# Layer 1's second set: second products by seven of eight instead of all eight

## The chip, the cores and the metric

The kernel runs on one core of a Trainium2 chip. The metric is the time of one execution on the device in microseconds (us); of several runs the median counts. The core's engines are TensorE (PE in the profile: matmuls; PEld: its weight loads), VectorE (DVE), ScalarE (ACT), GpSimd (POOL) and SyncE (SP), which here only issues transfers. Each engine works through its own queue in order and waits at an instruction whose operands are not there.

## The reference

A random-feature attention is followed by two gated layers:

```python
q_p, k_p = phi(q * scale), phi(k * scale)         # phi: exp(x @ omega.T - |x|^2/2 - max) / sqrt(m)
num = q_p @ (k_p.T @ v);  den = q_p @ k_p.sum(seq) + 1e-6
x = (num / den)                                   # 4 batches x 576 rows = 2304 rows, 8 heads x 64 = 512 columns
x = (silu(x @ w_gate) * (x @ w_val)) @ w_out      # layer 1: 512 -> 1536 -> 512
x = (sigmoid(x @ w_gate2) * (x @ w_val2)) @ w_out2  # layer 2, the same sizes
```

The weights come as float64 and are converted to float32 on the chip.

## The kernel before, in words

**Sets and stages.** Of the 2304 rows, 4 x 512 are handled as two *sets* of two batches each; the 4 x 64 rows left over ("R", 256 columns) go along with one set of each layer. Layers are numbered 0 and 1 in the code, so (0,0), (0,1), (1,0), (1,1) are (layer, set), in the order of the program (`LARGE`); (0,0) and (1,1) carry the leftover rows. In this text layer 1 of the title is layer 0 of the code. `big(l, n, ...)` does one set: six *blocks* p of 256 columns of d_ff, each of seven *slots* k (the first products, gate and value together), then the second products with w_out, then, for (0,0) and (1,1), twelve short slots of leftover rows.

**Seven of eight.** A product of 2 x 2 blocks needs eight block products; with sums of blocks formed beforehand on both sides (Strassen's scheme in Winograd's form) seven suffice. The first products of all four sets are done so: slots k0 to k6 accumulate in PSUM banks X, Z, X, Y, X, Z, X. For the second products there are two functions: `eight()`, twelve slots of 24 matmuls, and `seven()`, 21 slots; the tuple `SEVEN = (1, 0), (1, 1)` says which sets use `seven()`. There the left sums s1 to s4 of the hidden values are formed by `form_s1` to `form_s4` during the blocks before, and the right sums of w_out come from DRAM.

**Every product is three.** A float32 operand is split into a high part (ACT: `vh`, `xhi`, `hh`) and the rest (DVE: `vl`, `xlo`, `hl`), and `three` (L420 to L424) issues high x high, low x high, high x low.

**Weights.** Class `Weight` loads a 128 x 1024 piece of float64 words (`raw64`, by POOL's queue once attention is over) and turns it into float32: `magnitude` (L186, ACT), `bits` (L194), `power` (L201), `term` (L207) and `total` (L215, sometimes a POOL transfer instead), all DVE. A pair of pieces then gives block sums in `sums` (L273: four DVE operations 256 wide), and pieces and sums are stored to DRAM (`w_first`, `w_out`, `w_diff`) by SP. `make()` is this work as a generator. Later each slot fetches its 256 KB from there (`fetch`, SP, tile `wp`), three to five slots ahead, and splits it three slots ahead: `prepare_hi` (L407, ACT) and `prepare_lo` (L411, DVE).

**The order.** The program is written in the order in which each engine shall work. After the matmuls of each slot `step()` (L972) advances a clock, runs what `after(n, ...)` had put off, prepares the slot three ahead, and then takes conversions from `make()` according to a credit (`SHARES`, `room`, `needs`). At k4 and k5 `total` (L1021) adds PSUM sums on DVE, one slot later `gate` (L991) has ACT take the activation and DVE multiply. In the first block after a set whose second products go by `seven()`, the operand sums of x that are needed in slots 3 and later (`x_jobs`, `X_LATE`) are formed within that block; otherwise all of them are formed beforehand. Attention's order is a table of names, `START`.

Of the kernel before, what the change touches and what calls it, by code (L numbers as in the profile page):

```python
# [28 lines left out]
ld.0 mk.0 mq.0 nk.0 tK.0 tQ.0 hQ.0 hK.0 mr.0 ld.1 sr.0 load0.0 lv.0 tR.0 sk.0 hR.0 pK.0 pQ.0 mk.1  # L29
nq.0 lR.0 xK0.0 pR.0 mr.1 ld.2 gK0.0 bK0.0 xK1.0 gK1.0 bK1.0 mq.1 eK0.0 tK.1 sq.0 hK.1 load0.1 eK1.0  # L30
xQ0.0 nk.1 sk.1 gQ0.0 bQ0.0 xQ1.0 gQ1.0 tR.1 hR.1 bQ1.0 magnitude0.0 lv.1 sr.1 eQ0.0 load1.0 eQ1.0
pK.1 lR.1 magnitude1.0 kv.0 xK0.1 q0.0 bits0.0 tQ.1 q2.0 bits1.0 gK0.1 nq.1 bK0.1 ke.0 c0.0 pR.1
load1.1 c2.0 q1.0 mk.2 nA.0 hQ.1 xK1.1 tK.2 gK1.1 dA.0 load0.2 sq.1 lv.2 eK0.1 bK1.1 c1.0 hK.2 pQ.1
iA.0 power0.0 yA.0 power1.0 eK1.1 magnitude0.1 mr.2 mq.2 magnitude1.1 nB.0 xQ0.1 gQ0.1 nk.2 term1.0
bQ0.1 tR.2 sk.2 hR.2 sr.2 dB.0 ld.3 xQ1.1
# [20 lines left out]
LEAD = 3  # L56
EARLY_UNITS = 12
FULL = (4, 5, 6, None)
SPENT = 0.6
# [4 lines left out]
SEVEN = (1, 0), (1, 1)  # L64
X_LATE = 3
LEAD7 = 3

SHARES = ((1, 1, 1, 1), (1, 1, 1, 1), 0.2, 7)
# [8 lines left out]
def tile_performer_attention__then__two_glu_layers(  # L77
# [25 lines left out]
    nc = tc.nc  # L103
    P = 128
# [48 lines left out]
    class Weight:  # L153
# [36 lines left out]
        def bits(self):  # L190
            if self.cast:
                self.place()
                r = self.res.bitcast(U32)
                nc.vector.tensor_scalar(  # L194
                    r, self.mag.bitcast(U32), 3, None, ALU.logical_shift_left
                )

        def power(self):

            if self.cast:  # L200
                nc.vector.tensor_scalar(  # L201
# [9 lines left out]
        def total(self, dma=False):  # L211
            if self.cast and dma:
                nc.gpsimd.dma_start(out=self.res, in_=self.mag, accum_op=ALU.add)
            elif self.cast:
                nc.vector.tensor_tensor(self.res, self.res, self.mag, ALU.add)  # L215

    loader = [nc.sync]
    units = []
    for l in range(2):
        units += [Weight(l, c + i, n) for c in range(0, FC, 2) for n in range(2) for i in range(2)]  # L220
        units += [Weight(l, c, 2) for c in range(FC)]

# [5 lines left out]
    w_diff = dram.tile([P, 4, FC // 2, H2], F32, name="wd")  # L228
# [5 lines left out]
    def put(u, v=None, t=None):  # L234
# [12 lines left out]
        for at, src in (  # L247
# [5 lines left out]
            store(dst[:, at], src)  # L253

    def sums(u, v, t):
# [16 lines left out]
        for dst, l, r, op in right if u.key[2] == 2 else left:  # L272
            nc.vector.tensor_tensor(dst, l, r, op)  # L273
# [24 lines left out]
    for l, n, small in LARGE:  # L298
        for p in range(FC // 2):
            for slot, product, r in slots(l, n, small, p):  # L300
# [3 lines left out]
                vector.append(9 if full else 0.6 + {4: 1.8, 5: 1.8, 6: 0.6, None: 0.6}.get(product, 0))  # L304
# [25 lines left out]
    def x_sum(s, name, later):  # L330
# [8 lines left out]
        elif s == 1 and xt["late"]:  # L339
# [5 lines left out]
        for kk in range(2):  # L345
            nc.vector.tensor_tensor(t[kk], l[kk], r[kk], ALU.subtract)
# [1070 lines left out]
```

## Time and profile before

| | us |
|---|---|
| three runs | 983.75, 986.4, 989.13 (median 986.4) |
| the profiled execution: its time | 983.23 |
| its span (first to last instruction) | 981.3 |
| PE busy | 970.5 (99%) |
| DVE busy | 771.1 (79%) |
| ACT busy | 609.4 (62%) |
| POOL busy | 87.4 (9%) |

TensorE's granted clock is 1.000 over the whole span. The time of an execution is its span and some 2 us around it. A busy row says how long instructions of a group lasted, which is longer than the distance from one to the next where they follow each other closely, since an instruction's end overlaps the start of the next; the timeline with its start times tells the distance.

The stages by the trace's matmuls, in us from the span's start: attention to 163.6; (0,0) first products to 312.5, second products to 378.0, leftover rows to 395.3; (0,1) first products to 509.6, second products to 574.9; (1,0) first products to 689.1, second products to 750.75; (1,1) to the end.

### The profile page before, as it was taken

Reading aid. Unit: us, or ns where it says so; the run is one execution under the profiler, and the core shown is the slowest. Engines: PE = TensorE matmul, PEld = TensorE weight load, DVE = VectorE, ACT = ScalarE, POOL = GpSimd, SP = SyncE. Lnnn points to the kernel's source line nnn. Section 1 sums busy time; section 2 is a strip of 40 time slices with the busy share of each in tenths; the row PEclk is TensorE's granted clock in tenths of the full one; section 3 lists DMA queues with packets and bytes.
Section 4 is the critical chain, followed back from the end, with each engine's and each line's share of the span. In section 5 each row is a group of like instructions: output and inputs, shape, how many; then the busy total and the mean of one; then the engine's idle time right before and its main releaser. Section 6 shows DMA issues by size and latency. Waiting matters only on the chain.

```text
span 981.3 us, 16934 instructions
## 1 busy us (share of the span) xinstructions
PE 970.5 (99%) x5929; PEld 854.6 (87%) x5929; DVE 771.1 (79%) x1584; ACT 609.4 (62%) x1295; POOL 87.4 (9%) x130
## 2 busy tenths in 40 slices
PE   8999999999999999999999999999999999999998
PEld 7999998888888889888888888888999888889996
DVE  6898999888887899778888878856986655557674
ACT  7999998655554456555555465554775544445763
POOL 2222112011010100001000000000100000000200
PEclk9999999999999999999999999999999999999999
DMA  7657766577786666777765566543464322223754
GB/s 221 169 139 190 213 190 190 163 235 251 251 277 195 184 205 207 246 226 229 229 198 151 177 203 220 155 126 97 107 169 142 109 86 86 85 84 91 161 151 129
DMA packets 129913, 170.23 MB, mean 173 GB/s; under 512 B 32420, under 2 KB 83108, under 8 KB 129828
## 3 DMA queue, kind: packets, MB, share of 16 engines
q1 hardware_dynamic: 117392, 131.43, 44.3%
q0 software_dynamic: 11952, 37.49, 13.8%
q8 instruction: 46, 0.75, 0.3%
q14 instruction: 39, 0.32, 0.1%
q10 hardware_dynamic: 484, 0.23, 0.1%
HBM read 123.76 MB, written 39.32 MB: 166 GB/s over the span
## 4 chain that ended last, share of the span: by engine, by line
PE 92%; DVE 3%; ACT 2%; DMA 1%; issue 0%; ACTq 0%; SPq 0%; DVEq 0%
PE X L422 12%; PE X L424 12%; PE X L423 12%; PE Z L424 6%; PE Z L422 6%; PE Z L423 6%; PE Y L424 4%; PE Y L422 4%; PE Y L423 4%; PE p L644 3%; PE o L698 2%; PE R L424 2%; PE R L423 2%; PE R L422 2%; PE acc L422 2%; PE acc L423 2%
## 5 line engine op out<-in xcount | busy, mean ns | idle before, releaser
L411 DVE TENSOR_TENSOR vl<-wp,vh 128x512 fp32r<-128x512 f32 x274 | 188.2, 689 | 144.3 <-ACT vh L407 142.2
L407 ACT ACTIVATE vh<-wp 128x512 fp32r<-128x512 f32 x274 | 169.9, 623 | 7.8 <-PE X L424 3.1
L422 PE MATMUL X<-xhi,vh 128*128 128x512 f32 x372 | 145.2, 390 | 0.1
L423 PE MATMUL X<-xlo,vh 128*128 128x512 f32 x372 | 145.0, 390 | 0.0
L424 PE MATMUL X<-xhi,vl 128*128 128x512 f32 x372 | 144.7, 389 | 0.0
L424 PEld LDWEIGHTS X<-xhi,vl 128*128 128x128 f32 x372 | 69.8, 188 | 14.7
L422 PEld LDWEIGHTS X<-xhi,vh 128*128 128x128 f32 x372 | 69.9, 188 | 14.2 <-DVE o L1196 0.3
L423 PEld LDWEIGHTS X<-xlo,vh 128*128 128x128 f32 x372 | 69.9, 188 | 13.7
L422 PE MATMUL Z<-xhi,vh 128*128 128x512 f32 x184 | 71.6, 389 | 0.0
L423 PE MATMUL Z<-xlo,vh 128*128 128x512 f32 x184 | 71.6, 389 | 0.0
L424 PE MATMUL Z<-xhi,vl 128*128 128x512 f32 x184 | 71.6, 389 | 0.0
L994 ACT ACTIVATE g<-h 128x512 f32<-128x512 f32 x28 | 17.7, 632 | 64.5 <-DVE h L1024 64.5
L1019 ACT ACTIVATE Y<-X 128x512 f32<-128x512 f32 x52 | 30.2, 584 | 40.4 <-PE X L424 40.0
L424 PE MATMUL X<-vh,hl 128*128 128x256 f32 x192 | 54.4, 284 | 0.0
L424 PE MATMUL R<-xr,vl 128*128 128x256 f32 x192 | 54.3, 283 | 0.0
L423 PE MATMUL X<-vl,hh 128*128 128x256 f32 x192 | 54.3, 283 | 0.0
L422 PE MATMUL X<-vh,hh 128*128 128x256 f32 x192 | 54.3, 283 | 0.0
L423 PE MATMUL R<-xr,vh 128*128 128x256 f32 x192 | 54.3, 283 | 0.0
L422 PE MATMUL R<-xr,vh 128*128 128x256 f32 x192 | 54.2, 282 | 0.0
L207 DVE SCALAR_TENSOR_TENSOR mag<-raw,mag 128x512 f32<-128x512 uint32 x72 | 49.5, 688 | 1.2
L186 ACT ACTIVATE mag<-raw 128x512 f32<-128x512 f32 x72 | 48.6, 676 | 1.4 <-DMA raw<-in_moe_w_val_dram 1.1
L215 DVE TENSOR_TENSOR res<-res,mag 128x512 f32<-128x512 f32 x61 | 42.0, 688 | 1.0
(244 smaller groups left out, 2621.5 us busy)
## 6 DMA issues: line engine op xcount, KB each, us to landing
wp<-wf SPq DMA_DIRECT2D x184, 256.0 KB, 3.0
wp<-ws SPq DMA_DIRECT2D x66, 256.0 KB, 2.9
wf<-res SPq DMA_DIRECT2D x48, 256.0 KB, 3.7
wf<-wsums SPq DMA_DIRECT2D x48, 256.0 KB, 4.0
raw<-in_moe_w_out_dram POOLq DMA_DIRECT2D x24, 512.0 KB, 4.2
raw<-in_moe_w_gate_dram POOLq DMA_DIRECT2D x18, 512.0 KB, 5.1
raw<-in_moe_w_val_dram POOLq DMA_DIRECT2D x18, 512.0 KB, 4.4
ws<-res SPq DMA_DIRECT2D x24, 256.0 KB, 3.8
```

Of the source, the lines that this page charges most:

```text
L186: nc.scalar.activation(self.mag, self.hi.bitcast(F32), AF.Prelu, scale=REBIAS, alpha=NEGATIVE)
L207: nc.vector.scalar_tensor_tensor(self.mag, self.lo, 2.0**-52, self.mag, ALU.mult, ALU.mult)
L215: nc.vector.tensor_tensor(self.res, self.res, self.mag, ALU.add)
L407: nc.scalar.activation(hi, fetched[o], AF.Copy)
L411: nc.vector.tensor_tensor(lo, fetched.pop(o), hi.bitcast(F32), ALU.subtract)
L422: nc.tensor.matmul(o, lhsT=l[0], rhs=r[0], start=start, stop=False, **kw)
L423: nc.tensor.matmul(o, lhsT=l[0], rhs=r[1], start=False, stop=False, **kw)
L424: nc.tensor.matmul(o, lhsT=l[1], rhs=r[0], start=False, stop=stop, **kw)
L644: nc.tensor.matmul(pj[a][:, i, :], lhsT=x[hs, i, :], rhs=wdf[hs, a, :], start=True, stop=True)
L698: nc.tensor.matmul(self.kv[:, h], lhsT=lhsT, rhs=rhs, start=n == 0, stop=n == 2 * NB)
L994: nc.scalar.activation(g, src[0], AF.Sigmoid if l else AF.Silu)
L1019: nc.scalar.activation(d, s, AF.Copy)
```

## The change

`SEVEN` gets (0, 1), so layer 1's second set uses `seven()`: 21 slots of 12 matmuls 512 wide in place of 12 slots of 24. What this needs elsewhere:

- the right sums of layer 1's w_out: a class `Again` loads its twelve pieces (256 KB each) from DRAM once more by SP, two at a time, and makes four sums of each pair on DVE and stores them (24 operations, 12 stores); in program order this stands in slots s1 to s8 of (0,0)'s second products. `w_diff` exists once per layer;
- the left sums: `form_s1` becomes an ACT copy and an accumulating POOL transfer except in (1,1); `form_s2` and `form_s3` stay on DVE, `form_s4` a POOL transfer; results go into `xx`, the input of layer 2;
- conversions pause from block 4, slot 4 of (0,1) to the end of its second products (`PAUSE`), since `seven()` uses their tiles. What is due for layer 2 is done earlier or later;
- the x sums for slots 3 and later of (1,0) move into that set's first block;
- each DVE instruction is counted into an estimate of what VectorE still has to do (`Counted`, `ahead`); `step` takes conversions only where it is under `BACKLOG` = 7.0, and under `TIGHT` = 0.3 ahead of slot k4;
- `split` is divided: its DVE half comes after `step`; `total` for k4 and k5 stays ahead of it (`TOTAL_FIRST`);
- `START` is written anew, and the leftover rows of attention's first pair of heads (`kqrem`) are loaded by SP behind `qraw`, not by ACT's queue.

```diff
-SEVEN = (1, 0), (1, 1)
+SEVEN = (0, 1), (1, 0), (1, 1)
+TIGHT = {4: 0.3}
+S1_DMA = True
+PAUSE = 4, 4
+BACKLOG = 7.0
+TOTAL_FIRST = (4,5)
-SHARES = ((1, 1, 1, 1), (1, 1, 1, 1), 0.2, 7)
+SHARES = ((1,0.8,1,1),(1,1,1,1),0.2,7)
...
+            def call(out, *args, **kw):
...
+                quick = name in ("tensor_scalar", "tensor_copy")
+                ahead[0] += n / (1920.0 if quick else 960.0) + 0.07
+                return f(out, *args, **kw)
...
+        def load(self):
+            self.pair = []
+            for i in range(2):
+                u = Weight(0, self.c + i, 2)
+                u.place()
+                nc.sync.dma_start(out=u.res, in_=w_out[0][:, self.c + i])
+                self.pair.append(u)
...
-                    if self.n == 0 and n == 0:
+                    if self.n == 0 and n == 1:
                         for i, rest in enumerate((k, q)):
-                            nc.scalar.dma_start(out=self.r[:, i, :], in_=rest[0, :2, MAIN:, :])
+                            nc.sync.dma_start(out=self.r[:, i, :], in_=rest[0, :2, MAIN:, :])
...
+            while pausing and u not in begun_units:
+                yield "clean"
...
-        room.append(share * max(2.74 * x - SPENT * y, 0.1))
+        room.append((kind != "t" or l) and share * max(2.74 * x - SPENT * y, 0.1))
...
-        while credit >= 1:
+        ahead[0] = max(0.0, ahead[0] - 2.72 * weight[o - 1])
+        limit = BACKLOG
+        if o < len(sequence) and sequence[o][0] == "f" and sequence[o][3] in TIGHT:
+            limit = TIGHT[sequence[o][3]]
+        while credit >= 1 and ahead[0] < limit:
...
+            if S1_DMA and not (l and n):
+                nc.scalar.activation(s1[p], a21, AF.Copy)
+                nc.gpsimd.dma_start(out=s1[p], in_=a22, accum_op=ALU.add)
+                return
...
-                        for m in range(4):
+                        for i in range(2 - 2 * l):
+                            three(
+                                dst[i],
+                                [u[:, p % 2 * H2 + i * P:p % 2 * H2 + (i + 1) * P] for u in w],
+                                now,
...
+                        for m in range(4 * l):
...
+                    if k in (4, 5):
+                        t = hold[k - 3][i]
+                        vec.tensor_tensor(t if k == 4 and i else to, dst[i], t, ALU.add)
```

How the change moves instructions, at three places. In the changed kernel all operations of VectorE go through one wrapper and so have its line, L124.

SP's queue at the program's start (`kraw`, `qraw`: keys and queries of a pair of heads; `kqrem`: their leftover rows). Before:

```order
L540 DMA kraw_171<-in_k_dram 128x2x256
L540 DMA qraw_175<-in_q_dram 128x2x256
L540 DMA kraw_199<-in_k_dram 128x2x256
L540 DMA qraw_201<-in_q_dram 128x2x256
L549 DMA kqrem_170<-in_k_dram 64x3x64 x2
```

and now:

```order
L586 DMA kraw_172<-in_k_dram 128x2x256
L586 DMA qraw_174<-in_q_dram 128x2x256
L590 DMA kqrem_171<-in_k_dram 128x1x64
L590 DMA kqrem_171<-in_q_dram 128x1x64
L586 DMA kraw_187<-in_k_dram 128x2x256
L586 DMA qraw_189<-in_q_dram 128x2x256
```

The first pair's `kqrem` stands between the first and the second pair's large loads; before, it stood on ACT's queue, behind `omega`.

VectorE in (0,1), block 2, from behind the `vl` made in slot k4 to the one made in slot k5 (`res`, `mag`: conversion; `wsums`: block sums; `hs`: a left sum; `h`: hidden values). Before:

```order
L273 TENSOR_TENSOR wsums_6105<-res_5891,res_6021 128x256
L273 TENSOR_TENSOR wsums_6105<-res_5891,wsums_6104 128x256
L1024 TENSOR_TENSOR h_6068<-Z_5997,h_6068 128x512
L1024 TENSOR_TENSOR h_5879<-Z_5998,h_5879 128x512
L999 TENSOR_TENSOR h_5999<-g_6123,h_5999 128x512
L411 TENSOR_TENSOR vl_6151<-wp_6075,vh_6150 128x512
```

and now:

```order
L124 TENSOR_SCALAR mag_6152<-res_6154 128x512
L124 SCALAR_TENSOR_TENSOR mag_6152<-raw64_6088,mag_6152 128x512
L124 TENSOR_TENSOR res_6154<-res_6154,mag_6152 128x512
L124 TENSOR_TENSOR wsums_6209<-res_6120 128x256
L124 TENSOR_TENSOR wsums_6209<-wsums_6209,res_6057 128x256
L124 TENSOR_TENSOR hs_6001<-h_5728,h_5859 128x512
L124 TENSOR_TENSOR h_6134<-Z_6064,h_6134 128x512
L124 TENSOR_TENSOR h_5929<-Z_6065,h_5929 128x512
L124 TENSOR_TENSOR h_6066<-g_6194,h_6066 128x512
L124 TENSOR_TENSOR vl_6232<-wp_6145,vh_6231 128x512
```

Three conversion steps and a left sum have come in ahead of the totals from Z.

VectorE in (1,0), block 0, slots k2 and k3 (`xt`: operand sums of x, `xlo`: their low parts). Before:

```order
L201 TENSOR_SCALAR mag_7374<-res_7376 128x512
L207 SCALAR_TENSOR_TENSOR mag_7374<-raw64_7243,mag_7374 128x512
L411 TENSOR_TENSOR vl_7418<-wp_7324,vh_7417 128x512
L215 TENSOR_TENSOR res_7376<-res_7376,mag_7374 128x512
L273 TENSOR_TENSOR wsums_7426<-res_7240 128x256
L273 TENSOR_TENSOR wsums_7426<-wsums_7426,res_7327 128x256
L411 TENSOR_TENSOR vl_7445<-wp_7368,vh_7444 128x512
```

and now:

```order
L124 TENSOR_SCALAR mag_7494<-res_7496 128x512
L124 SCALAR_TENSOR_TENSOR mag_7494<-raw64_6560,mag_7494 128x512
L124 TENSOR_TENSOR xlo_7551<-xx_80,xhi_7549 128x512
L124 TENSOR_TENSOR xlo_7555<-xx_80,xhi_7553 128x512
L124 TENSOR_TENSOR vl_7558<-wp_7453,vh_7557 128x512
L124 TENSOR_TENSOR res_7496<-res_7496,mag_7494 128x512
L124 TENSOR_SCALAR res_7566<-mag_7564 128x512
L124 TENSOR_TENSOR xt_7580<-xx_80,xt_7161 128x512
L124 TENSOR_TENSOR xt_7580<-xx_80,xt_7162 128x512
L124 TENSOR_TENSOR xlo_7585<-xt_7580,xhi_7583 128x512
L124 TENSOR_TENSOR xlo_7589<-xt_7580,xhi_7587 128x512
L124 TENSOR_TENSOR vl_7594<-wp_7492,vh_7593 128x512
```

The sums of x and their splitting now stand in this block, and conversion runs beside them.

Counted over a whole block from the two listings, VectorE has these instructions (wide: 512, other than TENSOR_SCALAR; narrow: 256 wide, or a TENSOR_SCALAR 512 wide):

| block | before: wide + narrow | now: wide + narrow |
|---|---|---|
| (0,0) block 1 | 26 + 17 | 26 + 19 |
| (0,1) block 1 | 19 + 10 | 23 + 14 |
| (0,1) block 2 | 19 + 10 | 24 + 14 |
| (0,1) block 3 | 20 + 9 | 24 + 12 |
| (0,1) block 4 | 20 + 10 | 23 + 14 |
| (0,1) block 5 | 19 + 7, and 2 of 1024 | 20 + 4 |
| (1,0) block 0 | 18 + 11 | 32 + 6 |
| (1,0) block 1 | 24 + 9 | 23 + 14 |
| (1,0) block 2 | 22 + 9 | 24 + 13 |
| (1,0) block 3 | 18 + 2 | 24 + 13 |
| (1,0) block 4 | 18 + 0 | 20 + 10 |
| (0,0) second products | 52 + 27, and 11 of 1024 | 41 + 32, and 11 of 1024 |
| (0,1) second products | 49 + 28, and 10 of 1024 | 78 + 0 |

Two TENSOR_SCALARs stand for one conversion: before, (0,0)'s second products hold 18 of them and (0,1)'s first products 27; now 6 and 33.

## Rows read from the trace of the kernel before

**Rows 1.** The page: span, busy time of the engines, the chain by engine.

```profile
span 981.3 us, 16934 instructions
PE 970.5 (99%) x5929; PEld 854.6 (87%) x5929; DVE 771.1 (79%) x1584; ACT 609.4 (62%) x1295; POOL 87.4 (9%) x130
PE 92%; DVE 3%; ACT 2%; DMA 1%; issue 0%; ACTq 0%; SPq 0%; DVEq 0%
```

**Rows 2.** Windows by stage: length, busy us by engine, clock, DMA share, GB/s.

```profile
163.60:312.50 148.90, 148.27 (x789) 128.18 (x789) 130.47 (x245) 82.79 (x154) 14.61 (x22) 1.00 0.73 232
...
378.00:395.30 17.30, 17.30 (x146) 17.26 (x144) 15.85 (x29) 11.24 (x20) 1.50 (x2) 1.00 0.84 263
395.30:509.50 114.20, 114.20 (x506) 94.60 (x505) 93.49 (x172) 67.20 (x121) 10.53 (x14) 1.00 0.73 230
...
574.90:689.00 114.10, 114.10 (x505) 94.53 (x504) 85.30 (x149) 63.62 (x115) 2.33 (x4) 1.00 0.52 161
689.00:750.75 61.75, 61.62 (x506) 60.68 (x505) 51.52 (x84) 42.53 (x77) 5.21 (x6) 1.00 0.56 146
```

**Rows 3.** Windows: (0,1) block 2.

```profile
433.40:452.40 19.00, 19.00 (x85) 15.76 (x84) 15.85 (x31) 10.91 (x21) 1.57 (x2) 1.00 0.72 228
```

**Rows 4.** Timeline of PE: each stage's first matmul; at 602.50 (1,0) block 1, k3.

```profile
509.57 0.39 PE L422 MATMUL X<-hh,vh 128*128 128x512 f32 x1
...
574.85 0.39 PE L422 MATMUL X<-xhi,vh 128*128 128x512 f32 x1
...
602.50 0.39 PE L424 MATMUL Y<-xhi,vl 128*128 128x512 f32 x1
...
689.09 0.28 PE L422 MATMUL X<-vh,hh 128*128 128x256 f32 x1
...
750.75 0.50 PE L422 MATMUL X<-xhi,vh 128*128 128x512 f32 x1
```

**Rows 5.** Timeline of DVE in (1,0): start, duration; in brackets idle before and its end.

```profile
595.62 0.69 DVE L215 TENSOR_TENSOR res<-res,mag 128x512 f32<-128x512 f32 x1
596.23 0.42 DVE L194 TENSOR_SCALAR res<-mag 128x512 uint32<-128x512 uint32 x1
596.56 0.68 DVE L999 TENSOR_TENSOR h<-g,X 128x512 f32<-128x512 f32 x1
597.95 0.69 DVE L411 TENSOR_TENSOR vl<-wp,vh 128x512 fp32r<-128x512 f32 x1 [0.71 <-ACT vh L407]
598.56 0.42 DVE L201 TENSOR_SCALAR mag<-res 128x512 uint32<-128x512 uint32 x1
599.02 0.69 DVE L207 SCALAR_TENSOR_TENSOR mag<-raw,mag 128x512 f32<-128x512 uint32 x1
```

**Rows 6.** Waits over the span: us in total, times, longest.

```profile
DVE vl L411 <- ACT vh L407: 142.2, 105, 3.5
...
ACT g L994 <- DVE h L1024: 64.5, 28, 4.1
...
PE o L606 <- DMA kqrem<-in_q_dram: 1.3, 1, 1.3
PE t L606 <- ACT x_k L620: 1.0, 1, 1.0
```

**Rows 7.** The chain of waits at the start: start, length, what.

```profile
2.36 5.49 DMA kqrem<-in_q_dram
```

**Rows 8.** DMA issues of the first 9 us.

```profile
qraw<-in_q_dram SPq DMA_DIRECT2D x2, 256.0 KB, 4.2
```

**Rows 9.** Timeline of DVE behind the change from (1,0) to (1,1).

```profile
754.99 1.29 DVE L355 TENSOR_TENSOR xlo<-xx,xhi 128x512 fp32r<-128x512 f32 x2 [4.30 <-ACT xhi L359]
756.20 0.69 DVE L411 TENSOR_TENSOR vl<-wp,vh 128x512 fp32r<-128x512 f32 x1
```

**Rows 10.** DMA issues, whole span: count, KB each, median us to landing.

```profile
wp<-wf SPq DMA_DIRECT2D x184, 256.0 KB, 3.0
raw<-in_moe_w_gate_dram POOLq DMA_DIRECT2D x18, 512.0 KB, 5.1
```

More of the change, by code (lines that the diff above doesn't have):

```diff
@@ L221, in tile_performer_attention__then__two_glu_layers @@
         units += [Weight(l, c, 2) for c in range(FC)]
+        if l == 0 and (0, 1) in SEVEN:
+            units += [Again(c) for c in range(0, FC, 2)]
     dram = ctx.enter_context(tc.tile_pool(name="dram", bufs=1, space=bass.MemoryType.DRAM))
@@ L253, in put, with put_again @@
             store(dst[:, at], src)
+    def put_again(c, t):
+        for i in range(2):
+            store(w_diff[0][:, 2 * i:2 * i + 2, c // 2], t[i])
     def sums(u, v, t):
@@ L911, in make, with begin_unit @@
             put(u, v, t)
-        todo = None
+        todo, begun_units = None, set()
+        def begin_unit(u):
+            begun_units.add(u)
+            u.magnitude()
         for i, u in enumerate(units):
-            if i == 0:
-                u.magnitude()
+            if isinstance(u, Again):
+                if todo:
+                    yield from todo()
+                    todo = None
+                    u.load()
+                    yield
+                t = []
+                for x in units[i + 1:i + 2]:
+                    if isinstance(x, Again):
+                        x.load()
+                    else:
+                        units[i + 2].load()
+                        x.load()
+                yield from sums(*u.pair, t)
+                after(1, partial(put_again, u.c, t))
+                continue
+            while pausing and u not in begun_units:
+                yield "clean"
+            if u not in begun_units:
+                begin_unit(u)
                 yield
@@ L943, in make @@
                 todo = None
+            if stop and todo:
+                yield
+                yield from todo()
+                todo = None
         if todo:
@@ L1019, in copy, with total @@
             nc.scalar.activation(d, s, AF.Copy)
-    def total(l, h, left, t):
+    def total(l, h, left, t, now=False):
         for x, y in zip(left, t):
-            nc.vector.tensor_tensor(y, x, y, ALU.add)
-        after(1, lambda: gate(l, h, t))
+            vec.tensor_tensor(y, x, y, ALU.add)
+        if now:
+            gate(l, h, t)
+        else:
+            after(1, lambda: gate(l, h, t))
     def table(f):
@@ L1265, in big @@
                 step(1)
+                if k in (4, 5) and k not in TOTAL_FIRST:
+                    total(l, *((h2[1], X, h2) if k == 4 else (h1[1], Z, u2)), True)
+                if (p, k) == PAUSE and (l, n) == (0, 1) and (l, n) in SEVEN:
+                    pausing.append(1)
                 if k in (2, 4) and p and (l, n) in SEVEN:
@@ L1270, in big @@
                     if k == 3:
-                        for _ in making:
+                        while next(making, "clean") != "clean":
                             pass
```

193 lines of the change are left out of this document (122 added, 71 removed).

## The prediction

> **What bounds the kernel now.** The page comes first. TensorE is busy for 99% of the span and makes up 92% of the chain that ended last; VectorE, the next, is busy for 79% [rows 1]. So the time is the number of matmuls times their distance, plus what TensorE waits for. The windows by stage say where there is room: in the first products of (0,0) VectorE is busy for 130.5 of 148.9 us, with the leftover rows for 15.9 of 17.3, in those of (0,1) for 93.5 of 114.2, in those of (1,0) for 85.3 of 114.1 [rows 2]. The clock is at its full level in every one of them, so nothing is lost or won there. TensorE's wait rows are few: 1.3 us for `kqrem` and 1.0 us for ACT, both at the start [rows 6].
>
> How far ahead VectorE is, the timelines tell. In (1,0) it is idle for 0.71 us in front of a `vl` that starts at 597.95 and is done by 598.64; the first matmul that reads it, the third of slot k3, starts at 602.50 [rows 4, 5]. That is a lead of 3.9 us. Over the span VectorE waits 142 us in 105 pieces for the high part `vh` in front of `vl` [rows 6]: that idle time is the room which new work can fill for nothing. The lead is smaller after a set that used `seven()`: behind the change to (1,1) VectorE waits 4.30 us for `xhi`, and its `vl` starts at 756.20 [rows 9], while its slot k3 begins at 750.75 [rows 4] + 3 x 2.72 = 758.9 and reads it 0.45 us later. Lead there: 759.4 - 756.9 = 2.5 us.
>
> **Matmuls removed: -8.2 us.** (0,1)'s second products run from 509.57 to 574.85 [rows 4] with 12 x 24 = 288 matmuls of 512: 0.2267 us each. The change issues 21 x 12 = 252 of the same width. 36 x 0.2267 = 8.2 us, all on the path, since TensorE is busy throughout this stretch. New slots have their own seams: (1,0)'s second products take 689.09 to 750.75 = 61.7 us [rows 4] for 504 matmuls of 256 columns, where 0.12 us each gives 60.5. I take +0.9 of these 1.2 us for the new stage (0 to 1.2): the same operands, but a slot with half as many matmuls.
>
> **Start: -1.2 us.** `kqrem` is the first long piece of the chain: 5.49 us from its issue at 2.36 [rows 7], sharing the transfer engines with four large loads of SP, whose `qraw` has 4.2 us to landing [rows 8]. In SP's queue it now stands ahead of the second pair's two loads. At best TensorE's wait of 1.3 us [rows 6] goes; if queueing behind the first pair costs as much, nothing. Behind the start TensorE has no wait of that size [rows 6], so what is won stays won. I take -1.2, nearer to the upper end, since its two transfers are small and the two large ones that it used to share with are now behind it.
>
> **VectorE's added work: +4.6 us, the term that decides.** One wide operation to the next takes 595.62 to 596.23, 0.61 us; a narrow one 0.33 us; a narrow one whose result the next reads 0.46 us [rows 5]. For (0,1) block 2 the listing of before has 19 wide and 10 narrow: 19 x 0.605 + 10 x 0.335 = 14.9 us; the window of that block shows 15.85 busy [rows 3]. I add this 1.0 us (dependent neighbours, ends) to every block. A block's matmuls take 19.05 us (114.2 / 6, [rows 2]). With the counts of the table above:
>
> - (0,1): block 1 has 23 wide + 14 narrow = 18.6 + 1.0 = 19.6; block 2 20.2; block 3 19.5; block 4 19.6. Over TensorE's 19.05: 0.6 + 1.2 + 0.5 + 0.6 = 2.9 us, within the lead of 3.9. Block 5 has far less. Stall 0.
> - (0,1)'s second products: 78 wide = 47.2 of 57.1 us, room. `PAUSE` keeps conversion out, so nothing else stands there.
> - (1,0): block 0 has 32 + 6 = 21.4 + 1.0 = 22.4, 3.3 over; blocks 1 to 3 are 0.6 + 0.8 + 0.8 over; block 4 recovers. Together 5.5 us, against a lead of 2.5: stall **3.0**.
> - (0,0): 26 + 19 = 22.1 + 1.0 = 23.1 in blocks of 148.9 / 6 = 24.8: no sustained stall. But conversion comes in bursts: the listing of (0,1) block 2 shows ten operations where six stood, ahead of a `vl`; such a burst of 5 us in a slot of 2.72 eats most of the lead by itself. **0.5** for this stage.
> - Leftover rows of (0,0): 15.85 of 17.3 us before [rows 2], and the lead is thin. `Again`'s 24 sums (24 x 0.335 = 8 us) lie in the second products ahead of it, which lose conversion in exchange. **1.1.**
>
> Bounds: without the added 1.0 us per block, block 0 of (1,0) is 2.3 over and the others none, against 2.5: stall near 0.5 with the bursts. With as much again on top for the round trips through ACT and no lead left at a set's start, (0,1) gives 2.6, (1,0) 6.6 and (0,0) 3: 12 us. So +0.5 to +12.
>
> [...] Rows 5 show the next start 0.61 us after one that lasts 0.69, so for these shapes the overlap exists. [...]
>
> **Costed at nothing.** ACT's copies for s1 (ACT is busy 67 of 114 us in (0,1) [rows 2]) and the accumulating transfers on POOL's queue, behind raw loads that take 5.1 us to land [rows 10] and are issued a conversion ahead; the last s1 is formed with the first of the 42 products and read some seven products later, 7 x 6 x 0.2267 = 9.5 us. `Again`'s 12 loads and 12 stores (6.3 MB) stand in a stage from which six conversions have gone, each with 0.5 MB loaded and 0.25 MB stored (4.5 MB); on SP they stand between fetches that are needed three slots of 5.4 us later. In (0,1) conversions rise by a fifth (TENSOR_SCALARs 27 to 33): 230 GB/s [rows 2] becomes some 265; the leftover rows ran at 263 GB/s and a share of 0.84 without a wait of TensorE [rows 2].
>
> [...]
>
> **Sum** against the profiled execution's 983.2: - 8.2 + 0.9 - 1.2 + 4.6 = - 3.9, so 979.3. The median of the runs is 3.2 above the profiled execution, so the median after is forecast at **982.5 us**, -0.4%. A measurement of this kernel can tell some 0.5% (5 us) from no change: its three runs span 5.4 us.
>
> **Rivals.**
>
> - *VectorE keeps up.* Bursts are absorbed by the lead, because the held-back conversions leave k4 nearly empty (three operations and a `vl`), and block 0 of (1,0) starts with a full lead. Stall 0.8: 983.2 - 8.2 + 0.9 - 1.2 + 0.8 = 975.5, with 3.2 **978.7**. For it: 142 us of idle in front of `vl`. Against: block 0 of (1,0) is over by 2 us without any surcharge. It decides for this if a wide operation in a full queue keeps its 0.6 us and nothing dependent stands side by side.
> - *VectorE becomes the bound and the lateness comes back through ACT* (the other side). `gate` makes ACT wait for VectorE's totals (64.5 us in 28 waits, up to 4.1 [rows 6]); `vh` stands behind it in ACT's queue, and VectorE's next `vl` waits for `vh`. While there is a lead this costs nothing; once it is used up, VectorE idles in the very slots in which it is behind. At about 1 us more per block in the eight heavy blocks of (0,1) and (1,0), 2.9 + 5.5 + 8 = 16.4, less 3.9 and 2.5 of lead, gives 10, and bursts and the leftover rows of (0,0) 4 more: stall 14, 988.7, with 3.2 **991.9**. It takes over when a heavy block costs VectorE more than about 20 us.
> - *Transfers come late.* A fetch lands in 3.0 us [rows 10] and is issued three slots or more ahead, so some 5 us are spare. But SP works in order, and a store that waits for a late sum holds the fetches behind it. If in six heavy blocks one fetch is late by 1 us, 6 us come on top: **988.5**. Against: the 263 GB/s stretch without a wait.
> - *Every VectorE operation pays its full duration*: wide 0.69, narrow 0.42 [rows 5]. (0,1) is then over by 11.4 and (1,0) by 14.2, less the leads 19.2, plus 1.6: **998.7**. Against it: block 2 of (0,1) would have been busy for 17.3 us before; the window shows 15.85 [rows 3]. [...]
>
> **Chances.** Forecast 0.46 (its own range 979.5 to 986.5), VectorE keeps up 0.30, lateness through ACT 0.14, transfers 0.08, full durations 0.02. Faster by over 0.5% means 981.5 or less: 0.28 of the second case and 0.12 of the first, 0.40. Slower means 991.4 or more: 0.11 of the third, 0.02 each of the last two and of the forecast's end, 0.17. The rest, 0.43, lies within 0.5%. The range that holds eight in ten goes from the second case's 978.7 less half a run's scatter, 977, to the third case's lower half, 991.
>
> **What the profile of the changed kernel would show.** Right: the new stage takes 57 to 58.5 us against 65.3; `kqrem` lands near 6.5 and the first products of (0,0) start a microsecond earlier; TensorE's waits for `vl` total 3 to 7 us, most in (1,0) blocks 0 to 3; VectorE is above 95% busy there and `vl`'s idle in front for `vh` is far below 142 us. Wrong: waits of TensorE for `vl` above 10 us or spread over (0,1), then the third case; waits for `wp` in ACT's `vh`, then transfers; a stage of more than 60 us; or next to no waits of TensorE anywhere, then the second case.

## The result, and the profile after

The median of five executions of the changed kernel is 992.1 us (991.8 to 994.3), against 983.75 of the kernel before beside it: a ratio of 1.007, 95% interval 1.0046 to 1.0093. It is slower by 0.7%, and 1 us beyond the end of the stated range. The page of the profiled execution (991.8 us), span, busy times and chain:

```profile
span 990.0 us, 17171 instructions
PE 973.2 (98%) x5893; PEld 850.3 (86%) x5893; DVE 802.8 (81%) x1658; ACT 631.2 (64%) x1348; POOL 102.5 (10%) x148
PE 75%; DVE 13%; ACT 4%; issue 4%; DMA 2%; SPq 0%; DVEq 0%; ACTq 0%
```

Against [rows 1] TensorE's share of the chain fell from 92 to 75% and VectorE's rose from 3 to 13%. TensorE is busy for 2.7 us more, with 36 wide matmuls less: matmuls went slower at the start, at a lower clock (0.50), and behind each wait (starts 0.31 to 0.39 us apart instead of 0.23). The windows by stage (columns as in [rows 2]; boundaries are each stage's first matmul in the timeline) tell where:

```profile
167.73:317.18 149.45, 148.60 (x790) 128.11 (x789) 134.99 (x254) 84.05 (x156) 15.92 (x24) 1.00 0.75 242
317.18:402.34 85.16, 83.77 (x434) 71.24 (x433) 69.19 (x119) 43.59 (x70) 4.56 (x6) 1.00 0.65 202
402.34:519.72 117.38, 116.28 (x507) 94.06 (x505) 108.18 (x203) 69.64 (x131) 16.77 (x21) 1.00 0.87 270
519.72:578.58 58.86, 58.36 (x254) 46.91 (x252) 50.75 (x83) 44.20 (x79) 6.66 (x8) 1.00 0.55 140
578.58:698.14 119.56, 116.41 (x506) 93.90 (x504) 106.35 (x195) 72.03 (x134) 10.59 (x16) 1.00 0.68 211
```

The lengths of the stages, of this kernel and of those in the experiments (us; each from the one profiled execution, at its first matmuls):

| kernel | (0,0) begins at | (0,0) first | (0,0) second + leftover | (0,1) first | (0,1) second | (1,0) first |
|---|---|---|---|---|---|---|
| before | 163.60 | 148.91 | 82.79 | 114.27 | 65.28 | 114.24 |
| the change | 167.73 | 149.45 | 85.16 | 117.38 | 58.86 | 119.56 |
| start_old | 163.87 | 150.42 | 85.15 | 118.25 | 58.91 | 120.08 |
| kqrem_act | 167.01 | 149.46 | 85.16 | 117.99 | 58.86 | 120.12 |
| table_old | 166.56 | 150.28 | 85.13 | 118.11 | 58.87 | 120.47 |
| tight45 | 163.67 | 149.45 | 85.17 | 115.63 | 58.90 | 119.69 |
| fill | 163.75 | 149.45 | 85.17 | 115.47 | 58.87 | 118.71 |
| term_off | 166.52 | 149.57 | 84.69 | 114.27 | 58.85 | 115.50 |
| split_whole | 164.24 | 150.17 | 84.07 | 115.46 | 58.91 | 119.92 |
| fill_split | 164.03 | 149.42 | 84.06 | 115.37 | 58.89 | 119.18 |
| nodep | 164.34 | 149.42 | 84.08 | 115.85 | 59.07 | 119.50 |
| nopool_late | 164.44 | 149.38 | 83.76 | 118.82 | 58.92 | 119.25 |
| dma_total | 167.76 | 149.96 | 83.77 | 128.57 | 58.91 | 128.92 |
| best_pool | 164.04 | 149.40 | 85.05 | 124.85 | 58.86 | 126.70 |
| pool_late | 163.83 | 148.91 | 85.11 | 124.52 | 58.86 | 126.35 |
| seven_off | 163.85 | 148.93 | 86.33 | 114.27 | 70.16 | 114.24 |
| fill_before | 164.43 | 148.88 | 82.76 | 114.27 | 65.28 | 114.24 |

Rows whose program is the same in a stage differ from one another: by 0.5 to 0.9 us in (0,1), 1 us in (0,0)'s first products, 1.8 us in (1,0) (118.71 to 120.47). Differences of that size are not read.

So the change lost 4.1 us up to the first products, 0.5 (within the scatter) and 2.4 in (0,0), 3.1 in (0,1)'s and 5.3 in (1,0)'s first products, and won 6.4 in the second products it was made for and 0.6 behind: 8.4 us longer from first to last matmul.

At the start the windows show something that the profiled execution of the kernel before did not have, a lower granted clock:

```profile
8.00:10.00 2.00, 1.25 (x21) 1.06 (x20) 1.56 (x3) 1.43 (x3) 0.72 (x1) 1.00 0.50 113
10.00:12.00 2.00, 1.03 (x8) 0.77 (x8) 1.97 (x8) 1.72 (x6) 0.34 (x1) 1.00 0.61 138
12.00:14.00 2.00, 2.00 (x11) 1.61 (x13) 1.94 (x9) 1.92 (x9) 0.38 (x1) 0.52 0.87 263
20.00:22.00 2.00, 2.00 (x11) 2.00 (x10) 1.16 (x3) 1.15 (x3) 0.72 (x1) 0.50 0.62 182
22.00:24.00 2.00, 2.00 (x19) 1.83 (x19) 1.53 (x8) 1.78 (x7) 0.00 (x0) 0.92 0.80 259
```

TensorE is idle for 1.7 of the 4 us from 8 to 12, and from 12 to about 22 its granted clock is 0.50 to 0.52. TensorE's own timeline tells why it was idle, first before, then now:

```profile
7.98 0.30 PE L606 MATMUL o<-ident,kqrem 128*128 128x128 f32 x1 [1.27 <-DMA kqrem<-in_q_dram]
...
12.26 0.33 PE L606 MATMUL t<-ident,kqrem 128*128 128x128 f32 x1 [1.00 <-ACT x_k L620]
```

```profile
6.81 0.30 PE L652 MATMUL o<-ident,kqrem 128*128 128x128 f32 x1 [0.28 <-DMA kqrem<-in_q_dram]
...
9.84 0.39 PE L684 MATMUL r<-wd_hi,hi_r 128*128 128x256 f32 x1 [0.75 <-ACT hi_r L666]
...
11.96 0.40 PE L652 MATMUL t<-ident,kqrem 128*128 128x128 f32 x1 [0.97 <-ACT x_k L666]
```

`kqrem` came 1.2 us earlier, as forecast. TensorE then ran into two waits for ACT, a new one of 0.75 us and the old one for `x_k`, and the second pair's transpose begins at 11.96, only 0.3 us earlier than before. The waits of the kernel before were no shorter, yet its clock stayed full in this execution.

In (1,0) one stall, in three timelines (ACT, VectorE, TensorE; the bracket is idle time ahead):

```profile
641.36 0.63 ACT L1082 ACTIVATE g<-h 128x512 f32<-128x512 f32 x1 [4.04 <-DVE h L124]
641.90 0.61 ACT L453 ACTIVATE vh<-wp 128x512 fp32r<-128x512 f32 x1
```

```profile
637.40 0.42 DVE L124 TENSOR_SCALAR mag<-res 128x512 uint32<-128x512 uint32 x1
637.85 0.69 DVE L124 SCALAR_TENSOR_TENSOR mag<-raw,mag 128x512 f32<-128x512 uint32 x1
638.58 0.69 DVE L124 TENSOR_TENSOR res<-res,mag 128x512 f32<-128x512 f32 x1
639.19 0.42 DVE L124 TENSOR_TENSOR wsums<-res 128x256 f32<-128x256 f32 x1
639.64 0.42 DVE L124 TENSOR_TENSOR wsums<-wsums,res 128x256 f32<-128x256 f32 x1
639.98 0.69 DVE L124 TENSOR_TENSOR hs<-h 128x512 f32<-128x512 f32 x1
640.59 1.28 DVE L124 TENSOR_TENSOR h<-Z,h 128x512 f32<-128x512 f32 x2
641.78 0.68 DVE L124 TENSOR_TENSOR h<-g,h 128x512 f32<-128x512 f32 x1
```

```profile
642.57 0.50 PE L468 MATMUL Z<-xhi,vh 128*128 128x512 f32 x1 [1.17 <-ACT vh L453]
```

Read from the end: TensorE waits 1.17 us for `vh`; ACT's `vh` stands behind `g`; `g` waited 4.04 us for the total from Z; and VectorE did six operations of conversion and left sums, 3.2 us without a pause, ahead of that total. This is the chain of the rival *lateness through ACT*. (That this order is what makes the stage long is not shown by it; tight45 below tries that.) TensorE's wait rows sum it up, to be held against [rows 6], where none of these stood:

```profile
PE Z L468 <- ACT vh L453: 2.8, 6, 1.2
...
PE X L468 <- DVE h L124: 1.5, 2, 1.2
PE acc L469 <- DVE hl L124: 1.3, 2, 1.1
```

By block, the six of (1,0) take 1.5, 1.1, 0.2, 1.7, 0.8 and 0 us more than the 19.04 of the kernel before, those of (0,1) 0, 0, 0, 0.7, 1.5 and 0.9. Windows of (0,1) block 1 and of (1,0) blocks 0 and 3:

```profile
421.41:440.45 19.04, 19.04 (x85) 15.77 (x84) 18.51 (x36) 11.16 (x21) 3.19 (x4) 1.00 0.88 258
578.58:599.11 20.53, 19.30 (x85) 15.69 (x84) 16.02 (x28) 14.19 (x26) 0.56 (x1) 1.00 0.29 89
638.52:659.28 20.76, 19.59 (x85) 15.61 (x84) 20.35 (x40) 11.25 (x21) 2.55 (x4) 1.00 0.86 265
```

VectorE is 97% busy in (0,1) block 1 and TensorE loses nothing there yet, as with a lead that is used up first. In block 3 of (1,0) VectorE is 98% busy, in block 0 only 78%.

### The profile page after: what moved, and what is told of

It is laid out like the page before. It is cut to its first block, busy times and chain, and to the rows that moved or that the text cites. A ratio compares the mean times of both kernels' runs of the same rounds, so it can differ in the third digit from the quotient of the medians.

```text
span 990.0 us, 17171 instructions
## 1 busy us (share of the span) xinstructions
PE 973.2 (98%) x5893; PEld 850.3 (86%) x5893; DVE 802.8 (81%) x1658; ACT 631.2 (64%) x1348; POOL 102.5 (10%) x148
## 4 chain that ended last, share of the span: by engine, by line
PE 75%; DVE 13%; ACT 4%; issue 4%; DMA 2%; SPq 0%; DVEq 0%; ACTq 0%
PE X L469 9%; PE X L468 9%; PE X L470 9%; PE Z L470 5%; PE Z L468 5%; PE Z L469 5%; PE Y L470 4%; PE Y L469 4%; PE Y L468 3%; PE p L690 3%; PE o L744 3%; DVE vl L124 2%; PE R L470 2%; PE R L469 2%; PE R L468 2%
## 5 line engine op out<-in xcount | busy, mean ns | idle before, releaser
L124 DVE TENSOR_TENSOR vl<-wp,vh 128x512 fp32r<-128x512 f32 x283 | 194.3, 688 | 127.8 <-ACT vh L453 125.7
L453 ACT ACTIVATE vh<-wp 128x512 fp32r<-128x512 f32 x283 | 175.9, 625 | 10.3 <-DMA wp<-wf 4.0
L124 DVE SCALAR_TENSOR_TENSOR mag<-raw,mag 128x512 f32<-128x512 uint32 x72 | 49.5, 688 | 1.2
L468 PEld LDWEIGHTS Z<-xhi,vh 128*128 128x128 f32 x184 | 34.6, 188 | 12.0 <-ACT vh L453 5.3
```

The costliest lines, as they stand in the source:

```text
L124: return f(out, *args, **kw)
L453: nc.scalar.activation(hi, fetched[o], AF.Copy)
L468: nc.tensor.matmul(o, lhsT=l[0], rhs=r[0], start=start, stop=False, **kw)
```

## The experiments

The executions of the experiments, and those of the kernel before beside them, are each on record with their mean granted clock. Of the kernel before it was below 0.999 in 37 of 70 executions, with a median of 986.7 us against 983.5 of the other 33; of the change it was below in 5 of 5.

**The start: start_old, kqrem_act, table_old, tight45.** The first undoes the whole start, the second and the third one half of it each; tight45 leaves the start and holds conversions back ahead of slot k5 too.

```diff
 start_old: START as in the kernel before, and
-                    if self.n == 0 and n == 1:
+                    if self.n == 0 and n == 0:
-                            nc.sync.dma_start(out=self.r[:, i, :], in_=rest[0, :2, MAIN:, :])
+                            nc.scalar.dma_start(out=self.r[:, i, :], in_=rest[0, :2, MAIN:, :])
 kqrem_act: these two lines alone; table_old: START alone
 tight45:
-TIGHT = {4: 0.3}
+TIGHT = {4: 0.3, 5: 0.3}
```

> The change with the start of the kernel before: its START table, and kqrem of the first pair on ACT's queue. The profile of the change shows the granted clock at half its level from about 12 to 22 us and the first products of (0,0) beginning at 167.7 instead of 163.6. Theory 1 (the new start order costs the clock): clock 1.000 throughout, first products begin at 163.4 to 163.8, time 4 to 5 us below the change. Theory 2 (the clock fell by chance or for another reason than the start): the clock falls again, time within 1 us of the change.

> The change with only kqrem of the first pair back on ACT's queue; the new START table stays. If the queue of kqrem alone costs the clock (the first pair is ready early and TensorE then waits for the second): clock 1.000, first products begin near 163.5. If the new table alone does it: clock low for some 10 us again and first products near 167.5.

> The change with only the old START table; kqrem stays on SP's queue between the two pairs' loads. If the table costs the clock: 1.000 and first products begin between 162.4 and 163.6, that is the 1.2 us that I had forecast. If the queue of kqrem does: low clock again, near 167.5.

> The change with conversions also held back ahead of the totals of slot k5, as they are for k4 (TIGHT for 4 and 5). The same instructions, another order on VectorE. Theory A (the burst of conversion ahead of the Z totals makes ACT's gate late, and vh behind it): TensorE's waits for vh and for h in (0,1) and (1,0) fall to less than half, first products of (0,1) from 117.4 to 115 to 116 us, those of (1,0) from 119.6 to 116 to 117.5, time 4 to 6 us below the change. Theory B (VectorE has more work per block than TensorE, wherever it stands): the waits move to other slots, and the two stages stay within 1 us of 117.4 and 119.6.

Measured: start_old 990.1 us (ten executions, ratio 1.0057, 1.0039 to 1.0076), the clock at 0.999 or above in 6 of 10; those end at 988.8 to 990.4, the other four at 992.3 to 993.5. Like with like, the change with the old start is 6 us slower than the kernel before at either clock (989.3 against 983.5, 993.1 against 986.7). kqrem_act 992.2 and table_old 993.1 (one execution each) had the low clock: 0.73 and 0.62 already from 14 to 16 us. tight45, with the change's own start, had it in 9 of 10, but not in the profiled one. Its (0,0) then begins at 163.67, the kernel before's 163.60. So the clock falls by chance, and the whole new start worsens the odds: 14 of 15 with it (the change and tight45), 4 of 10 with the old one. Which half does it is not shown, since one low execution each says little where the kernel before has low ones in half of its own. At full clock the new start wins nothing.

For VectorE tight45 gave theory A its due in (0,1): 117.4 to 115.6 us. In (1,0) the stage stayed (119.7), as theory B has it. TensorE's wait rows of tight45 tell how:

```profile
PE X L468 <- DVE h L124: 2.9, 4, 1.2
PE X L470 <- DVE vl L124: 0.8, 2, 0.5
```

The waits for ACT's `vh` are gone, and in (1,0) waits for VectorE itself, for `h` and `vl`, have taken their place. The time is 989.2 (1.0046, 1.0032 to 1.0061); my 4 to 6 us below the change were 2.9.

**Is it TensorE's pause? fill.** tight45 with redundant matmuls in the pauses:

```diff
-                for i in range(n):
+                again = {("k", 1): 2, ("r", 1): 4}.get((key, self.n), 1)
+                for i in list(range(n)) * again:
                     nc.tensor.transpose(tp[:, i, :], x[:, i * P:(i + 1) * P], ident)
...
-                for i in range(NB):
+                again = 2 if self.n == 0 and key == "q" else 1
+                for i in list(range(NB)) * again:
                     for a, hs in enumerate(halves):
                         nc.tensor.matmul(
```

> tight45 with redundant matmuls at the start: the first pair's projection of q is done twice, the second pair's transposes of k twice and those of its leftover rows four times, which puts about 1.9 us of TensorE work into the stretch from 8 to 13 us where it stands idle for some 2 us. In tight45 the granted clock was below 0.999 in 9 of 10 executions, with the same new start in all of them (the change: 5 of 5; the old start 4 of 10, the kernel before 7 of 19). Theory 1 (the clock falls because TensorE pauses at the start): the clock stays at 0.999 or above in at least 7 of 10 executions, and these end 2.5 to 3.5 us earlier than the rest. Theory 2 (the clock falls for another reason): still below in 8 or more of 10, and the time is that of tight45, 989, or up to 1 us more.

Measured: 0.999 or above in 10 of 10, median 985.9 us (985.1 to 986.6) where tight45 had 989.2: 3.4 us. Its windows:

```profile
8.00:10.00 2.00, 2.00 (x38) 1.90 (x35) 1.64 (x6) 1.34 (x5) 0.73 (x1) 1.00 0.49 110
10.00:12.00 2.00, 1.52 (x13) 1.26 (x11) 1.50 (x6) 1.24 (x5) 0.36 (x1) 1.00 0.63 141
12.00:14.00 2.00, 1.74 (x18) 1.42 (x19) 1.87 (x9) 2.00 (x9) 0.36 (x1) 1.00 0.89 272
```

**VectorE's load or the transfers? term_off, dma_total.** On tight45:

```diff
 term_off, in Weight.term:
-            if self.cast:
+            if self.cast and self.key[0] == 1:
+                ahead[0] += 512 / 960.0 + 0.07
+            elif self.cast:
                 vec.scalar_tensor_tensor(
 dma_total:
     def by_dma(l, c, n):
-        return False
+        return l == 1
```

> tight45 without one VectorE operation of 0.6 us (the product L207 of the kernel before) in each conversion of layer 2's weights, the rest in the same order; the weights of layer 2 come out other than the reference's. Some 3 operations less per block in (0,1) and (1,0). Theory B (in (1,0) VectorE has more work than TensorE has time): the first products of (1,0) go from 119.7 to 115 to 117 us, those of (0,1) from 115.6 to 114.3 to 115. Theory C (transfers, now 250 to 310 GB/s, hold up the fetches): their number is the same, so both stages stay within 0.7 us.

> tight45 with the last step of each conversion of layer 2's weights (the sum L215 of the kernel before, 0.6 us of VectorE) as an accumulating transfer on POOL's queue instead, the result unchanged. Theory B: first products of (1,0) from 119.7 to 115 to 117 us as without the product, time 986 to 987.5 at a median clock like tight45's. Theory C: more transfers, so (0,1) and (1,0) get longer, by 1 us or more each.

Measured: term_off has (0,1) at 114.27, to the hundredth the stage of the kernel before, and (1,0) at 115.5. Windows of the two stages:

```profile
400.78:515.05 114.27, 114.27 (x507) 94.60 (x505) 97.83 (x185) 70.35 (x130) 16.24 (x20) 1.00 0.88 271
573.90:689.40 115.50, 114.52 (x506) 94.52 (x504) 97.52 (x181) 72.29 (x133) 10.39 (x16) 1.00 0.71 218
```

TensorE waits for nothing in (0,1) at 271 GB/s and a DMA share of 0.88, the transfers of the change. It is the amount on VectorE: 98 us busy in place of 108.2 and 106.4. Theory C falls. What (1,0) still has over the 114.24 of before, 1.3 us, all lies in block 0 (20.30 us, the other five 19.04), at one wait. VectorE's row ahead of it and TensorE's row:

```profile
590.53 1.28 DVE L124 TENSOR_TENSOR h<-X,h 128x512 f32<-128x512 f32 x2
591.36 0.47 PE L470 MATMUL X<-xhi,vh 128*128 128x512 f32 x1 [0.98 <-DVE h L124]
```

Slot k6 may not overwrite bank X before VectorE has added k4's total from it, and that total stands behind the sums of x and their low parts (`xt`, `xlo`), which the change moved into this block. The change has the same wait at 596.29, 1.2 us. No run puts these sums back, so that it is they is read from the order, not shown.

dma_total was a clear miss: 1009.9 us (1.025, 1.0205 to 1.0295), (0,1) 128.6 and (1,0) 128.9. Longer stages are what theory C forecast, but late fetches are not the reason: ACT waits 4.1 us for them in (0,1), where the change has 3.3, and not at all in (1,0). VectorE's own wait rows:

```profile
DVE wsums L124 <- DMA res<-mag: 24.8, 14, 4.3
```

The operation left VectorE, and VectorE waited for the transfer that took its place, with `vl` queued behind the block sums: 24.8 us in 14 waits.

**The low half of split: split_whole, seven_off.** The first undoes that one edit on top of tight45, the second undoes the seven products alone and keeps every other edit of the change.

```diff
 split_whole:
-                    hs[c + 2] = split_hi(h[c + 2], c)
+                    hs[c + 2] = split(h[c + 2], c)
...
-                if c + 2 < FC:
-                    split_lo(h[c + 2], hs[c + 2])
 seven_off:
-SEVEN = (0, 1), (1, 0), (1, 1)
+SEVEN = (1, 0), (1, 1)
```

> tight45 with the VectorE half of split back ahead of step in (0,0)'s second products, so that no conversion stands ahead of hl. Second products and leftover rows of (0,0) take 85.2 us in the change against 82.8 before, with one wait of TensorE of 1.1 us for hl at 377.7. If the moved half makes hl late: 83.3 to 84 us, and the wait for hl is gone. If VectorE is simply full there: 84.7 to 85.3, with the wait elsewhere.

> The change with SEVEN as before, so (0,1)'s second products take all eight and no sums of layer 1's w_out are remade; every other edit stays (start, split, holding back of conversion). If the longer stages of (0,0) come from those edits: second products and leftover rows still near 85 us, first products 149.5. If from remaking the sums: 82.8 to 83.3 and 148.9. (0,1) and (1,0) first products 114.2 to 114.6, second products of (0,1) 65.3.

Measured: with split whole, second products and leftover rows of (0,0) take 84.07 us, 1.1 less, and the wait of 1.1 us for `hl` is gone. In seven_off the first products of all three sets are those of the kernel before within 0.03 us; so the longer ones come with the seven products and what they add, not from the start, the counting or the holding back alone. But (0,0)'s second products with the leftover rows take 86.3 and (0,1)'s eight 70.2 instead of 65.3. TensorE's wait rows of it:

```profile
PE X L469 <- DVE hl L124: 2.6, 4, 0.9
PE acc L469 <- DVE hl L124: 2.4, 2, 1.3
```

Both are `hl`, which now stands behind conversions. I had expected 65.3 there; the one execution of seven_off takes 991.7 us, at the full clock, so the other edits cost more than they bring where the seven products are missing.

**Mends: fill_split, nodep, nopool_late, best_pool, pool_late, fill_before.** fill_split is tight45, fill and split_whole together, and the base of the next four; fill_before is the kernel before with fill's diff.

```diff
 nodep, in Weight.power:
-                vec.tensor_scalar(
-                    self.mag.bitcast(U32), self.res.bitcast(U32), 0xFF800000, None, ALU.bitwise_and
-                )
+                m = self.mag.bitcast(U32)
+                vec.tensor_scalar(m, m, 3, 0xFF800000, ALU.logical_shift_left, ALU.bitwise_and)
 nopool_late, pool_late:
-LATE_COST = 1.5
+LATE_COST = 3.0
 best_pool, pool_late, in sums:
-            vec.tensor_tensor(dst, l, r, op)
+            (nc.gpsimd if u.key[0] == 1 else vec).tensor_tensor(dst, l, r, op)
```

> The change with tight45, fill and split_whole together, LATE_COST as in the change: control for nodep. Stages as in the single mends: second products and leftover rows of (0,0) 83.8 to 84.1 us, (0,1) near 115.5, (1,0) 118.7 to 119.9; time 984 to 985.5.

> fill_split with one edit: power takes its bits from mag with a shift and a mask in one operation, not from the res that bits has written just before; result and number of operations are unchanged. Rows of before show 0.46 us from bits to power where the second reads the first and 0.33 where not; there are three to four conversions per heavy block. If such neighbours are a good part of the excess: (1,0) 1.5 to 2.5 us below fill_split, (0,1) 0.5 to 1, time 981.5 to 983.5. If the order hides them or the excess is elsewhere: both stages within 0.5 us of fill_split.

> The change with four mends: conversions held back ahead of k5's totals too (tight45), the extra matmuls at the start (fill), the low half of split ahead of step (split_whole), and LATE_COST 3.0 instead of 1.5, which moves some three conversion steps from block 0 of (1,0), the heaviest, to blocks 1 to 4; VectorE's work over the stage is the same. Theory B with the sum over the stage deciding: (1,0) keeps 117.5 to 119 of fill's 118.7 us, because blocks 1 to 3 now lack what block 0 gains. If only the peak in block 0 counted: 115 to 116. Time 982.5 to 985 at the full clock.

> tight45, fill and split_whole together, and the block sums of layer 2's weights (four operations of 256 per pair, 0.34 us each on VectorE) on GpSimd. In blocks 1 to 4 of (0,1) and (1,0) VectorE's operations of a block fall from 18.5 to 19.2 us to 15.8 to 17.1. Theory B: (0,1) 114.3 to 115, (1,0) 115.5 to 117 us, time 979.5 to 982. Against it: GpSimd and VectorE may hinder each other, and GpSimd's queue also issues the raw loads, so that a late sum holds up a load, and SP's store of the sum a fetch; then both stages get longer than fill's 115.5 and 118.7.

> best_pool with LATE_COST 3.0, so that block 0 of (1,0), which has no block sums to give away, has 18.8 us of VectorE operations instead of 21.2, and blocks 1 to 4 no more than 17.1. Theory B: (1,0) 114.3 to 115.5 us, the first version in which no block asks for more than TensorE's 19.05; time 978 to 981 and below the kernel before.

> The kernel before with the same extra matmuls at its start and nothing else. If TensorE's pauses at the start cost the clock there too: at 0.999 or above in at least 8 of 10 executions (of the kernel before itself 19 of 32), and a median of 983 to 984.5; without effect: the same share of low ones as before, and a median of 985 to 987.

*fill_split*: 985.0 us, ratio 0.9997 (0.9985 to 1.0009), the full clock in 10 of 10: as fast as the kernel before and no faster.

*nodep*: a miss. 985.3 us, both stages within 0.5 us. VectorE's timeline shows the pair of operations no closer:

```profile
640.17 0.42 DVE L124 TENSOR_SCALAR res<-mag 128x512 uint32<-128x512 uint32 x1
640.62 0.43 DVE L124 TENSOR_SCALAR mag<-mag 128x512 uint32<-128x512 uint32 x1
```

0.45 us from one to the next (the median of all 36 such pairs), the dependent pair's distance [rows 5]: the second no longer reads what the first writes, but overwrites what the first reads.

*nopool_late*: 987.4 us (1.0021, 1.0005 to 1.0037). (1,0) is at 119.25, as expected from a sum that stays; the peak in block 0 alone would have given 115 to 116. (0,1), where I expected no change, grew by 3.4 to 118.8, with VectorE busy as long as in fill_split (108.2 us). The program shares the pace of conversion out over both stages, so its order there moved too. One wait there lasted 2.55 us, and the clock fell once more, far from the start:

```profile
473.89 0.47 PE L468 MATMUL X<-xhi,vh 128*128 128x512 f32 x1 [2.55 <-DVE h L124]
```

and its windows right there:

```profile
470.00:474.00 4.00, 1.45 (x7) 0.90 (x7) 1.77 (x4) 0.22 (x1) 0.00 (x0) 1.00 1.06 339
474.00:478.00 4.00, 4.00 (x12) 3.20 (x13) 3.97 (x7) 1.98 (x4) 0.00 (x0) 0.64 0.79 277
```

*best_pool* and *pool_late*: misses, 1003.2 (1.0178, 1.0152 to 1.0204) and 1000.6 us (1.0149, 1.0124 to 1.0173). VectorE has 35 operations less in (0,1) than in fill (168 against 203 in the stage's windows) and is busy for 111.6 us instead of 108.1. GpSimd's and VectorE's timelines of best_pool in (0,1):

```profile
432.78 1.08 POOL L318 TENSOR_TENSOR wsums<-wsums,res 128x256 f32<-128x256 f32 x1
433.48 1.05 POOL L318 TENSOR_TENSOR wsums<-res 128x256 f32<-128x256 f32 x1
434.17 1.03 POOL L318 TENSOR_TENSOR wsums<-res,wsums 128x256 f32<-128x256 f32 x1
```

```profile
432.89 2.88 DVE L124 TENSOR_TENSOR vl<-wp,vh 128x512 fp32r<-128x512 f32 x1 [0.31 <-ACT vh L453]
```

One `vl`, 0.69 us elsewhere, lasts 2.88 us, from the first of these three sums of GpSimd to just behind the end of the last. Sixteen of VectorE's 512-wide operations last over 1 us in this stage, none in fill's.

*fill_before*: 984.3 us (983.7 to 984.5), the full clock in 10 of 10, ratio 0.9985 (0.9973 to 0.9997): the best complete version that was run, by little (term_off, which leaves out a product, had 983.0). (Until then the kernel before had 0.999 or above in 17 of 32 executions, not in 19 as the expectation says.) The kernel before itself loses 3.2 us in about half of its executions, and filling the pauses at its start ends that.

## Why the prediction was wrong

The step that failed is the term that was to decide, VectorE's added work: it let a lead of 3.9 us pay for lateness that is not paid that way, and was mis-sized at +4.6 us where 11.3 were measured. The start failed beside it: a gain of 1.2 us that did not come, and a clock taken for constant.

- **VectorE's added work, +4.6, measured 11.3** (0.5 + 2.4 + 3.1 + 5.3), within the bounds of 0.5 to 12 that I gave it. The mechanism was right, the sizes were not, in these places. *(0,1), 0 forecast, 3.1 measured*: I set the sum over blocks, 2.9 us, against a lead of 3.9. tight45 shows that 1.75 us of it came from the order within slot k5: the six operations ahead of Z's totals. I saw the burst in the listing and gave it 0.5 in (0,0) alone. The other 1.4 are amount: without one product per conversion the stage is back at 114.27. *(1,0), 3.0 forecast, 5.3 measured*: here the amount decides, since the order changed no more than the scatter and term_off took off 4.2 us. But it did not fall where I put it. I had block 0 over by 3.3 us and block 4 recovering; VectorE is busy for only 78% of block 0, which loses 1.5 us at one wait, and blocks 1 to 4 lose 3.8 between them. *Second products and leftover rows of (0,0), 1.1 forecast, 2.4 measured*: 1.1 is `split`'s low half behind the conversions, an edit that I named and did not cost. The rest, 1.3, is open; in split_whole 1.0 of it lies in the leftover rows (18.33 us against 17.35), where I had put the term.
- **The start, -1.2, measured +4.1.** "Behind the start TensorE has no wait of that size, so what is won stays won" failed twice. [rows 6] itself had the wait of 1.0 us for `x_k`, which lies behind `kqrem`; when TensorE came 1.2 us earlier, ACT's `hi_r` and `x_k` were what it waited for, and at full clock (tight45) nothing was left of the gain. (The full wait rows also have one of 1.8 us for POOL's `vr`, longer than the two I named; it is the same in both kernels.) And "the clock is at its full level, so nothing is lost or won there" took one profiled execution for the rule: 37 of 70 executions of the kernel before have a lower mean clock. That filling the pauses keeps the clock up is shown by fill, 10 of 10 against 1 of 10, and by fill_before, 10 of 10 beside 8 of 19; the loss is 3.2 to 3.4 us. In my own base the two readings even met: every execution of the kernel before at 986 us or above whose clock is on record had the lower one, so the 3.2 us by which I put the median above the profiled execution fit this same loss, and it was no constant to add.
- **The matmuls, -8.2 + 0.9, measured -6.4.** The new stage takes 58.86 us, 1.7 above its 252 matmuls; my seams were 0.9. "57 to 58.5" missed by 0.4.
- **The rivals.** *Lateness through ACT* is the chain that the three timelines show, but it is not the cause of (1,0)'s length: tight45 ended the waits for `vh` and the stage stayed, with VectorE itself late. That its 991.9 is near 992.1 is luck: it has 11.3 us where I priced it at 14, and the clock does the rest. I gave it 0.14 because I let the lead pay for everything; a lead pays for a sum, not for a total that is late in its own slot. *Transfers*: excluded by term_off, and no `vh` in (1,0) waited for a fetch; the one that did in (0,1) (3.3 us, at 403.5) had no wait of TensorE behind it. *Full durations*: excluded; the full queue of the change starts wide operations 0.6 us apart (640.59, two of them, to 641.78). So does [rows 5]: 0.61 us from a wide start to the next.
- **What would show it wrong.** "Waits of TensorE for `vl`" was too narrow: they came as waits for `vh`, `h` and `hl`, 2.8, 1.5 and 1.3 us in the rows. Most of the rest lies in the few matmuls right behind each wait, which start 0.31 to 0.39 us apart instead of 0.23.

## What to carry to other kernels

Where an engine is to be filled as far as VectorE here (97% of (0,1) block 1, 98% of (1,0) block 3), count its work per block, but look also at what stands ahead of each result that another engine waits for: the same instructions in another order were worth 1.8 us in one stage here, and nothing beyond the scatter in another, where the amount was too much in any order. Before work is moved off a full engine, ask what it will share with the new place: a transfer and GpSimd both made it worse by more than the whole change (dma_total 20.7 us above tight45, best_pool 18.2 above fill_split, the change 8.3 above the kernel before). And compare the granted clock of every execution, not of the profiled one alone, before reading a start or a median.

## What the runs showed of the hardware

- TensorE's granted clock fell in some executions of one kernel and not in others: the mean of the execution was below 0.999 in 37 of 70 of the kernel before and in 9 of 10 of tight45. At the start of the change it was 0.50 to 0.52 from 12 to 22 us, behind 1.7 us of idle time between 8 and 12; in nopool_late a wait of 2.55 us from 471 was followed by 4 us at a mean of 0.64. Redundant matmuls in the pauses of the start kept the mean clock at 0.999 or above in all forty executions of fill, fill_split, nodep and fill_before.
- With the block sums on GpSimd (best_pool) a `vl` of VectorE lasted 2.88 us beside three of them, 0.69 elsewhere; the three took 1.03 to 1.08 us, where GpSimd's operations of the same size in the change's attention take 0.73.
- In nodep a TENSOR_SCALAR of VectorE that only overwrites what the one before it reads started 0.45 us after it (median of 36 pairs), where [rows 5] has 0.33 for neighbours without a tie.
